# Attention and gated FFN on one core: whole-batch loads, attention by token tile over all heads, full-array matmuls, two-bank PSUM tiles, output tiles across batch pairs

## The chip, the cores and the metric

The kernel runs on one core of one Trainium2 chip. The metric is the device time of one execution in microseconds (us). The kernel before takes 329.29 us (median of 2 runs, 328.94 to 329.65). Every experiment below was timed beside runs of the kernel before on its own chip; those medians were 328.36, 329.02, 328.94 and 328.63 us, so the yardstick moves by 0.2%.

The engines are called as the profile calls them: PE is TensorE (matmuls), PEld its weight loads, ACT is ScalarE, DVE is VectorE, POOL is GpSimd, SP is SyncE. In both kernels matmuls write into tiles in the memory called PSUM, and an ACT or DVE instruction then moves each result into SBUF, where the other tiles lie; that instruction is called an eviction here. A two-bank tile is a PSUM tile of 2 x 512 float32 columns.

## The reference, cut to what matters

Eight batches, eight heads, 576 tokens, head size 64. K and V are averaged over groups of 8 tokens (72 pooled tokens), attention is taken over those, and a gated FFN with a convolution of three taps follows.

```python
k_p = k.reshape(B, H, 72, 8, 64).mean(axis=3)          # V likewise
attn = softmax(q @ k_p.T / 8)                          # 576 x 72 for each head
x = (attn @ v_p) joined over heads                     # 576 x 512
h = relu(x @ w_in)                                     # 576 x 1024
c = conv3(h, conv_w)                                   # along tokens, one filter per column
out = (h * sigmoid(c)) @ w_out                         # 576 x 512
```

## The kernel before

While the FFN of batch b runs, the attention of batch b+1 is woven between its blocks. The heads go in pairs. Each q row lands with token `c*96 + p` on partition p, so the transposed q has its tokens in order. A score matmul contracts over 64 rows (one head), between FFN matmuls that use all 128.

```python
def attn_loads(b, pr):
    ...
        for hh in range(2):
            nc.gpsimd.dma_start(
                out=q_sb[:, :, hh, :],
                in_=q[b, h0 + hh, :, :].rearrange("(c p) d -> p c d", p=96),
            )

def attn_scores(b, pr):
    ...
    for c2 in range(n_sc):              # two halves of 288 tokens
        c0 = c2 * SC
        for hh in range(2):
            pb = hh * D
            scps = sc_psum.tile([Sp, SC], FP32, name="scps", tag="sc")
            nc.tensor.matmul(
                out=scps,
                lhsT=kT_sb[pb:pb + D, :],            # 64 rows x 72 columns
                rhs=qT_sb[pb:pb + D, c0:c0 + SC],
                start=True, stop=True,
            )
            nc.scalar.activation(
                out=attnTs[hh][:, c0:c0 + SC], in_=scps, func=ACT.Exp, scale=1.0 / (POOL * 8.0)
            )

# the FFN: 16 times 4 matmuls of 288 columns (hps, relu by ACT), 16 times 3 (cps, tanh by ACT),
# then five output tiles of 128, 128, 128, 128 and 64 tokens, 8 matmuls of 512 columns each
... (the rest cut)
```

The softmax here doesn't subtract the row's maximum and nothing guards it: scores larger than these inputs give would overflow.

## Time and profile before

| read from | value |
|---|---|
| median time | 329.29 us (328.94 to 329.65) |
| span of the profiled execution | 327.8 us |
| PE busy | 289.7 us, 88% of the span |
| chain of waits, share of PE | 79% |
| one steady batch | 35.80 us, of which PE is busy 35.1, DVE 26.0, ACT 22.4 |

The table of stretches, for two steady batches (a third is equal) (from, to: length, then the busy time and count of PE, PEld, DVE, ACT and POOL, the granted TensorE clock, the busy share of the DMA engines and GB/s):

```profile
124.70:160.50 35.80, 35.06 (x259) 20.11 (x259) 25.79 (x113) 22.42 (x58) 12.21 (x23) 1.00 0.61 84
160.50:196.30 35.80, 35.21 (x265) 20.25 (x263) 26.05 (x114) 22.38 (x58) 12.50 (x24) 1.00 0.62 84
```

PE is busy for 98% of a batch. That is no proof that it does useful work all that time. The timeline of PE in one of these batches shows what a score matmul costs; the first number of a line is the start in us, the second the duration, and because matmuls overlap it is the distance between starts that counts.

```profile
128.28 0.28 PE L273 MATMUL hps<-xT,w_in_sb_116 128*128 128x288 bf16 x1
128.57 0.28 PE L191 MATMUL scps<-qT_sb,kT_sb 64*72 64x288 bf16 x1
128.79 0.30 PE L273 MATMUL hps<-xT,w_in_sb_117 128*128 128x288 bf16 x1
128.92 0.29 PE L273 MATMUL hps<-xT,w_in_sb_118 128*128 128x288 bf16 x1
```

Two 128-row matmuls in a row start 0.13 us apart (128.79, 128.92). With a 64-row score matmul between them they start 0.51 us apart (128.28, 128.79). PE counts as busy through all of it.

### The profile page before, as it was taken

To read this page: it belongs to the slowest core of one execution; us is meant where nothing else is said; L and a number is where in the kernel's file an instruction comes from. 1 tells how busy PE (TensorE), PEld (TensorE's weight loads), DVE (VectorE), ACT (ScalarE), POOL (GpSimd) and SP (SyncE) were. 2 spreads that over 40 slices of the span, in tenths; PEclk is the share of its full clock that TensorE was granted. 3 is DMA by queue.
4 is the path that set the end of the run, shared out by engine and by line. 5 is a ranking of instruction groups with operands and counts; after the bars stand their busy time and mean duration, and the time that the engine had idled before them with its cause. 6 is when DMAs were issued, how large, how long until landed. Compare 5 with 4: busy or idle time off the path is not lost.

```text
span 327.8 us, 6104 instructions
## 1 busy us (share of the span) xinstructions
PE 289.7 (88%) x2080; PEld 166.7 (51%) x2080; DVE 213.5 (65%) x904; ACT 188.3 (57%) x473; POOL 103.0 (31%) x196
## 2 busy tenths in 40 slices
PE   0054669999999999999999999999999999999995
PEld 0032335664566446654656456554566455645752
DVE  3523883677857785778757785777667866675452
ACT  1068425883398509872587429860787348852940
POOL 8068997752442226042513233110000000000000
PEclk9999999999999999999999999999999999999999
DMA  8999999995693659155964567133100120003003
GB/s 166 173 120 190 150 151 129 147 104 98 125 100 22 84 123 109 31 54 97 135 79 36 82 138 56 8 27 108 40 2 1 66 81 2 0 34 112 2 32 113
DMA packets 57342, 27.28 MB, mean 83 GB/s; under 512 B 42464, under 2 KB 51552, under 8 KB 57312
## 3 DMA queue, kind: packets, MB, share of 16 engines
q0 software_dynamic: 51968, 17.20, 48.2%
q10 hardware_dynamic: 2928, 5.38, 4.9%
q1 hardware_dynamic: 2416, 4.33, 4.5%
q8 instruction: 16, 0.26, 0.3%
q14 instruction: 14, 0.11, 0.1%
HBM read 32.52 MB, written 9.44 MB: 128 GB/s over the span
## 4 chain that ended last, share of the span: by engine, by line
PE 79%; DMA 11%; ACT 3%; DVE 3%; POOL 2%; issue 1%; ACTq 0%; POOLq 0%
PE hps L273 22%; PE cps L293 15%; PE scps L191 8%; DMA q_sb<-in_q_dram 5%; PE avps L223 5%; PE xt_ps L252 3%; PE q_ps L173 2%; DMA convw<-in_moe_conv_w_dram 2%; ACT xT L255 2%; DMA k_raw<-in_k_dram 2%; DMA w_in_sb_119<-in_moe_w_in_dram 1%; DVE osb L336 1%; DMA out_dram<-osb 1%; PE kT_ps L162 1%; DVE x_pair L234 1%
## 5 line engine op out<-in xcount | busy, mean ns | idle before, releaser
L234 DVE TENSOR_SCALAR x_pair<-avps,r_sb 128x64 bf16<-128x64 f32 (+1 forms) x320 | 72.3, 275 | 0.5
L293 PE MATMUL cps<-hT,dw 128*128 128x288 bf16 x384 | 60.3, 288 | 0.0
L255 ACT COPY xT<-xt_ps 128x576 bf16<-128x576 bf16 x32 | 20.4, 637 | 69.0 <-PE xt_ps L252 56.9
L121 POOL DMA_DIRECT2D q_sb<-in_q_dram x64 | 47.9, 759 | 35.7 <-PE q_ps L173 22.5
L231 DVE RECIPROCAL r_sb<-avps 128x2 f32<-128x2 f32 (+1 forms) x160 | 22.9, 161 | 54.4 <-PE avps L223 53.7
L198 ACT ACTIVATE attnT<-scps 72x288 bf16<-72x288 f32 x128 | 51.0, 405 | 12.8 <-PE scps L191 9.5
L280 ACT ACTIVATE hT<-hps 128x288 bf16<-128x288 f32 x128 | 52.0, 413 | 8.1 <-PE hps L273 3.7
L300 ACT ACTIVATE tg<-cps 128x288 bf16<-128x288 f32 x128 | 48.7, 412 | 7.4 <-PE cps L293 7.1
L191 PE MATMUL scps<-qT_sb,kT_sb 64*72 64x288 bf16 x128 | 39.1, 318 | 5.4 <-ACT attnT L198 4.8
L223 PE MATMUL avps<-v_aug,attnT 72*128 72x65 bf16 (+1 forms) x320 | 37.9, 202 | 5.3 <-DVE x_pair L234 4.2
L328 PEld LDWEIGHTS <-gT 128*128 128x128 bf16 (+1 forms) x320 | 27.8, 99 | 26.0 <-DVE gT L321 1.8
L293 PEld LDWEIGHTS <-dw 128*128 128x128 bf16 x384 | 35.3, 98 | 9.7 <-issue 0.2
L223 PEld LDWEIGHTS <-attnT 72*128 72x128 bf16 (+1 forms) x320 | 26.4, 102 | 26.0 <-issue 9.7
L273 PE MATMUL hps<-xT,w_in_sb_116 128*128 128x288 bf16 x128 | 37.5, 295 | 2.3 <-DVE osb L336 1.4
L273 PE MATMUL hps<-xT,w_in_sb_119 128*128 128x288 bf16 x128 | 36.4, 293 | 3.1 <-ACT xT L255 3.1
L273 PE MATMUL hps<-xT,w_in_sb_118 128*128 128x288 bf16 x128 | 37.5, 295 | 0.4 <-ACT xT L255 0.4
L273 PE MATMUL hps<-xT,w_in_sb_117 128*128 128x288 bf16 x128 | 37.4, 294 | 0.4 <-ACT xT L255 0.4
L178 ACT COPY qT_sb<-q_ps 128x576 bf16<-128x576 bf16 x32 | 20.5, 640 | 25.3 <-PE q_ps L173 25.1
L147 POOL MEMSET v_aug<- 72x2 bf16 x32 | 3.3, 110 | 100.2 <-PE avps L223 99.8
L191 PEld LDWEIGHTS <-kT_sb 64*72 64x72 bf16 x128 | 13.4, 109 | 29.2 <-issue 23.1
L252 PE MATMUL xt_ps<-ident_b,x_pair 128*128 128x128 bf16 (+1 forms) x160 | 26.5, 224 | 0.1
L113 POOL DMA_DIRECT2D v_raw<-in_v_dram x28 | 19.8, 707 | 11.5 <-DVE vt_3488 L149 2.6
(719 smaller groups left out, 429.3 us busy)
## 6 DMA issues: line engine op xcount, KB each, us to landing
q_sb<-in_q_dram POOLq DMA_DIRECT2D x64, 72.0 KB, 3.8
out_dram<-osb ACTq DMA_DIRECT2D x16, 256.0 KB
k_raw<-in_k_dram POOLq DMA_DIRECT2D x28, 144.0 KB, 4.5
v_raw<-in_v_dram POOLq DMA_DIRECT2D x28, 144.0 KB, 4.3
out_dram<-osb SPq DMA_DIRECT2D x8, 256.0 KB
out_dram<-osb POOLq DMA_DIRECT2D x8, 256.0 KB, 2.4
v_raw<-in_v_dram ACTq DMA_DIRECT2D x4, 288.0 KB
k_raw<-in_k_dram SPq DMA_DIRECT2D x4, 288.0 KB
```

What stands on the lines that cost most here:

```text
L121: nc.gpsimd.dma_start(out=q_sb[:, :, hh, :], in_=q[b, h0 + hh, :, :].rearrange("(c p) d -> p c d", p=96),)
L191: nc.tensor.matmul(out=scps, lhsT=kT_sb[pb:pb + D, :], rhs=qT_sb[pb:pb + D, c0:c0 + SC], start=True, stop=True,)
L198: nc.scalar.activation(out=attnTs[hh][:, c0:c0 + SC], in_=scps, func=ACT.Exp, scale=1.0 / (POOL * 8.0))
L223: nc.tensor.matmul(out=avt[0:usz, sl, hh, :], lhsT=attnTs[hh][:, u0:u0 + usz], rhs=v_aug[:, hh, :], start=True, stop=True,)
L234: nc.vector.tensor_scalar(out=x_pair[0:usz, hh * D:(hh + 1) * D], in0=avt[0:usz, sl, hh, 0:D], scalar1=r_sb[0:usz, hh:hh + 1], scalar2=Non ...
L252: nc.tensor.transpose(out=xt_ps[:, u0:u0 + usz], in_=x_pairs[i][0:usz], identity=ident_b[0:usz, 0:usz])
L255: nc.scalar.copy(out=xT, in_=xt_ps)
L273: nc.tensor.matmul(out=hps, lhsT=w_in_sb[dc][:, fb * P:(fb + 1) * P], rhs=xT_tiles[(b, dc)][:, c0:c0 + SC], start=(dc == 0), stop=(dc == n ...
L280: nc.scalar.activation(out=hT[:, fb, 1 + c0:1 + c0 + SC], in_=hps, func=ACT.Relu, scale=0.5)
L293: nc.tensor.matmul(out=cps, lhsT=dw[:, kk, i, :], rhs=hT[:, fb, c0 + kk:c0 + kk + SC], start=(kk == 0), stop=(kk == 2),)
L300: nc.scalar.activation(out=tg[:, c0:c0 + SC], in_=cps, func=ACT.Tanh, scale=0.5)
L328: nc.tensor.matmul(out=ops_[0:osz, :], lhsT=gT[:, fc, os0:os0 + osz], rhs=w_out_sb[fc], start=(fc == 0), stop=(fc == n_fb - 1),)
```

## The change

The intent is to give PE nothing but full-array matmuls and to give the other engines fewer and larger instructions.

- q, k and v of a whole batch come in one DMA each. For q, six consecutive tokens go to one partition (token `p*6 + c`), so a descriptor moves 1,536 contiguous bytes of float32 instead of 256.
- Keys are padded with zeros to 128 rows, and q is transposed two tokens at a time, so a score matmul is 128 rows deep. Its output is in the order of q's partitions; the exp puts the tokens back in order as it writes.
- Relu, tanh and exp evict 576 columns at once from two-bank PSUM tiles. Attention by V goes by token tile over four heads at a time; the last tile overlaps the one before, so that every tile has 128 tokens.
- Output tiles run over the 1,152 tokens of two batches: 9 full tiles in place of 10.
- The convolution's diagonal weights and the copies of the transposed q and x move from ACT to DVE, and every other output copy from DVE to ACT.

The core of the diff (cut; lines of the old and the new score function, the q load and the output tile):

```diff
-                in_=q[b, h0 + hh, :, :].rearrange("(c p) d -> p c d", p=96),
+    q_view = "h (p c) d -> p h c d"
+        nc.gpsimd.dma_start(out=qr, in_=q[b].rearrange(q_view, c=QC))
 ...
-                    lhsT=kT_sb[pb:pb + D, :],
-                    rhs=qT_sb[pb:pb + D, c0:c0 + SC],
-                nc.scalar.activation(
-                    out=attnTs[hh][:, c0:c0 + SC], in_=scps, func=ACT.Exp, scale=1.0 / (POOL * 8.0)
+        ps = big_psum.tile([P, 2, 512], FP32, name="sc_ps", tag="big")
+        for c2 in range(2):
+            nc.tensor.matmul(
+                out=ps[0:Sp, c2, 0:SC],
+                lhsT=kz[b % 2][:, h, c2, :],
+                rhs=qT[:, h % 2, :],
+        at = attnT_pool.tile([Sp, S], BF16, name="attnT")
 ...
+            nc.scalar.activation(
+                out=at.rearrange("s (p cp c2) -> s c2 cp p", cp=QC // 2, c2=2),
+                in_=ps[0:Sp, :, 0:SC].rearrange("s c2 (cp p) -> s c2 cp p", cp=QC // 2),
+                func=ACT.Exp,
+                scale=1.0 / (POOL * 8.0),
+            )
 ...
+                lhsT=gT[:, fb, j * P:(j + 1) * P],       # gT holds 2 * 576 tokens
+        tiles = range(0, 4) if b % 2 == 0 else range(4, 9)
 ... (the rest cut)
```

The output of the exp: token `p*6 + cp*2 + c2`, with p running fastest.

## The prediction

> **What bounds it now.** The chain of waits is 79% TensorE work. In time order it shows about 50 us of start-up, seven batches of 35.8 us (FFN of b, attention of b+1), and a last batch without attention of 22 us plus 3.6 us of tail. In a steady batch the table by stretches shows PE busy 35.1 of 35.8 us, DVE 26.1, ACT 22.4, clock 1.00; the waits list has 3.6 us of PE idle in six batches. TensorE bounds it.
>
> **Where the 35.8 us go.** In the timeline a 288-column matmul follows another every 0.123 us, a 512-column one every 0.216, a 128-column transpose every 0.058, a q transpose every 0.042. Dense, a batch costs 7.84 (first FFN matmul) + 5.88 (conv) + 8.64 (five output tiles) + 1.97 (scores) + about 3.8 of small work = 28 us. About 7.7 is lost: a score matmul on a 64-row tile between 128-row ones costs about 0.35 us, and 64-wide tails about 0.1 us at each change. The Trainium skill (TensorEngine Tiling, Key Properties) says that changing the tiling mode drains the engine; the trace agrees, about 60 changes x 0.11 us.
>
> **Per batch, after.** All matmuls take the full array, so about 6.6 us of changes goes. Output tiles: 4.5 in place of 5, -0.86 us. PE sum: 26.9 us (4 tiles) or 28.6 (5), mean 27.7. ACT: 24 evictions of 576 columns at about 0.65 us (the 576-column copy took 0.637) plus half the output copies: 17 us. DVE, from about 0.15 us fixed plus columns: trees 5.9, q copies 1.8, normalising 10 x 0.58, x copies 2.1, gate 8 x 0.77, output 1.5: 23 us. That is below PE but near it while AV runs, with two one-bank buffers for everything small: I allow 1.3 us of new waits, so about 29 us.
>
> **Start-up.** q descriptors of 256 B become 1,536 B. FFN 0 could begin near 30 us instead of 50. But the built order puts later trees early on DVE: K of batch 2 stands ahead of the last xT copy of batch 0, and K, V up to batch 5 ahead of batch 1. At about 330 GB/s read (estimate from packet durations), K of batch 2 lands near 45 us, and batch 0 is then paced by loads and eight trees. Most of the gain is given back: batch 1 starts near 80 us in place of 87.
>
> **Sum.** 80 + 6 x 29 + 22 + 3.6 = 280 of span; timed runs are 1.5 us above the span. Predicted **283 us**, range 268 to 302. Chances: faster by over 2% 0.96, within 2% 0.03, slower 0.01.
>
> **What would show it.** Right: steady period 28 to 30 us; scores on 128-row tiles at 0.123 us spacing; no 64-wide tiles; PE idle of 1 to 2 us per batch, released by DVE or ACT; DVE idle before trees released by DMA in the first 80 us. Wrong: period above 31 us with PE waiting for DVE or ACT (the two-buffer pool, or slow PSUM copies); or batch 1 near 60 us (loads faster than estimated, or the trees do not hold back FFN 0).
>
> **What would make it wrong.** bf16 copies from PSUM at half the assumed rate add 3 us of DVE per batch; three two-bank buffers shared by first matmul, conv and scores make PE wait for ACT; strided exp output slower than 0.65 us; the load rate.

## More of the kernel before

The page first. Its first part gives each engine's busy time and share of the span; part 4 is the chain of work that ended last; part 5 has groups of instructions, with the busy time in us and the mean time of one in ns after the first bar.

```profile
span 327.8 us, 6104 instructions
PE 289.7 (88%) x2080; PEld 166.7 (51%) x2080; DVE 213.5 (65%) x904; ACT 188.3 (57%) x473; POOL 103.0 (31%) x196
...
PE 79%; DMA 11%; ACT 3%; DVE 3%; POOL 2%; issue 1%; ACTq 0%; POOLq 0%
...
L198 ACT ACTIVATE attnT<-scps 72x288 bf16<-72x288 f32 x128 | 51.0, 405 | 12.8 <-PE scps L191 9.5
...
L191 PE MATMUL scps<-qT_sb,kT_sb 64*72 64x288 bf16 x128 | 39.1, 318 | 5.4 <-ACT attnT L198 4.8
```

The last work is almost all PE's, and ACT is on 3% of the chain only. The exps take 405 ns each, two for a head.

## The result, and the profile after

The changed kernel takes **356.49 us** (356.00 to 356.97, 2 runs). It is slower: the ratio to the kernel before is 1.083, with a 95% interval of 1.078 to 1.088. Ratios here are the mean time of one kernel's fast runs over that of the other's of the same rounds, so not quite the ratio of the medians that are quoted.

The same parts of the page, after:

```profile
span 355.1 us, 5143 instructions
PE 264.0 (74%) x2049; PEld 169.0 (48%) x2049; DVE 176.3 (50%) x497; ACT 210.4 (59%) x209; POOL 26.4 (7%) x55
...
ACT 40%; PE 37%; DVE 14%; issue 5%; DMA 3%; ACTq 0%
...
L182 ACT ACTIVATE attnT<-sc_ps 72x576 bf16<-72x576 f32 x64 | 128.0, 2216 | 13.4 <-PE sc_ps L165 13.4
...
L245 ACT ACTIVATE hT<-h_ps 128x576 bf16<-128x576 f32 x64 | 48.1, 754 | 36.9 <-PE h_ps L238 36.9
...
L265 ACT ACTIVATE tg<-c_ps 128x576 bf16<-128x576 f32 x64 | 41.9, 654 | 8.4 <-PE c_ps L257 4.7
```

PE's busy time did fall, by 26 us, and DVE's by 37. ACT was on 3% of the chain and is on 40% now. Three evictions of 576 columns stand side by side in part 5: relu 754 ns, tanh 654 ns, and exp 2,216 ns. The exp has the fewest partitions of the three.

Two steady batches in the table of stretches (the mean of six is 39.75 us, read from the first convolution matmul of each batch in the timeline):

```profile
132.34:171.09 38.75, 31.01 (x255) 20.10 (x253) 20.23 (x56) 25.99 (x26) 0.96 (x3) 0.96 0.19 43
171.09:211.56 40.47, 32.95 (x262) 20.81 (x261) 18.75 (x55) 26.01 (x26) 0.94 (x3) 0.96 0.19 48
```

No engine is busy for more than 82% of the batch, and ACT for two thirds only (25.99 of 38.75, 26.01 of 40.47). A share over the batch hides the stage that limits. The scores of the eight heads stand in four of the FFN's steps, two heads in each, and there the timelines of ACT and PE look as follows.

```profile
250.97 0.65 ACT L265 ACTIVATE tg<-c_ps 128x576 bf16<-128x576 f32 x1
251.51 4.00 ACT L182 ACTIVATE attnT<-sc_ps 72x576 bf16<-72x576 f32 x2
255.13 0.87 ACT L245 ACTIVATE hT<-h_ps 128x576 bf16<-128x576 f32 x1
255.88 0.65 ACT L265 ACTIVATE tg<-c_ps 128x576 bf16<-128x576 f32 x1
...
253.65 0.90 PE L257 MATMUL c_ps<-hT,dw 128*128 128x288 bf16 x6 [0.84 <-ACT attnT L182]
...
255.56 0.89 PE L165 MATMUL sc_ps<-qT,kz_107 128*72 128x288 bf16 x4 [0.76 <-ACT attnT L182]
```

A step takes 4.9 us (tanh at 250.97, the next at 255.88), ACT has no gap in it, and PE waits twice, 0.84 and 0.76 us, for an exp to free a PSUM buffer. The list of PE's waits over six batches (what waited, for what, us in total, times, longest) agrees:

```profile
PE c_ps L257 <- ACT attnT L182: 17.6, 21, 0.8
PE sc_ps L165 <- ACT attnT L182: 14.3, 18, 1.0
PE av_ps L195 <- ACT attnT L182: 5.5, 6, 1.0
```

The start-up pays as well: the chain of waits holds the first eight exps as one piece of 15.5 us.

So the question was what makes an exp of 576 columns take 2.2 us. Theory T1: the write, 2-byte elements 12 bytes apart. Rivals: the four-dimensional access pattern itself (T2), the stepped read or the two-bank source, and, for the time as a whole, the start-up alone or the change's pools.

### The profile page after: what moved, and what is told of

It reads as the page before. It is cut to its first block, busy times and chain, and to the rows that moved or that the text cites. A ratio compares the mean times of both kernels' runs of the same rounds, so it can differ in the third digit from the quotient of the medians.

```text
span 355.1 us, 5143 instructions
## 1 busy us (share of the span) xinstructions
PE 264.0 (74%) x2049; PEld 169.0 (48%) x2049; DVE 176.3 (50%) x497; ACT 210.4 (59%) x209; POOL 26.4 (7%) x55
## 4 chain that ended last, share of the span: by engine, by line
ACT 40%; PE 37%; DVE 14%; issue 5%; DMA 3%; ACTq 0%
ACT attnT L182 32%; PE o_ps L277 17%; PE h_ps L238 9%; PE c_ps L257 7%; ACT tg L265 4%; DVE x L206 4%; DMA v_126<-in_v_dram 3%; ACT hT L245 3%; PE av_ps L195 2%; DVE gT L271 2%; DVE o L288 2%; PE xt_ps L219 1%; DVE xT L221 1%; DVE r L205 1%; PE q_ps L152 1%
## 5 line engine op out<-in xcount | busy, mean ns | idle before, releaser
L182 ACT ACTIVATE attnT<-sc_ps 72x576 bf16<-72x576 f32 x64 | 128.0, 2216 | 13.4 <-PE sc_ps L165 13.4
L238 PE MATMUL h_ps<-xT,w_in_sb 128*128 128x288 bf16 x512 | 84.6, 304 | 2.0 <-DVE xT L221 0.5
L257 PE MATMUL c_ps<-hT,dw 128*128 128x288 bf16 x384 | 62.5, 295 | 20.3 <-ACT attnT L182 19.9
L245 ACT ACTIVATE hT<-h_ps 128x576 bf16<-128x576 f32 x64 | 48.1, 754 | 36.9 <-PE h_ps L238 36.9
L277 PE MATMUL o_ps<-w_out_sb,gT 128*128 128x512 bf16 x288 | 65.6, 382 | 5.7 <-DVE o L288 4.1
L238 PEld LDWEIGHTS <-w_in_sb 128*128 128x128 bf16 x512 | 49.6, 102 | 19.5 <-issue 5.9
L265 ACT ACTIVATE tg<-c_ps 128x576 bf16<-128x576 f32 x64 | 41.9, 654 | 8.4 <-PE c_ps L257 4.7
L277 PEld LDWEIGHTS <-gT 128*128 128x128 bf16 x288 | 27.6, 98 | 39.1 <-issue 6.0
L288 DVE COPY o<-o_ps 128x512 f32<-128x512 f32 x20 | 13.8, 691 | 44.2 <-PE o_ps L277 44.2
L206 DVE TENSOR_TENSOR x<-av_ps,r 128x256 bf16<-128x256 f32 x80 | 33.5, 419 | 0.8
L158 DVE COPY qT<-q_ps 128x576 bf16<-128x576 bf16 x32 | 14.6, 457 | 31.4 <-PE q_ps L152 31.0
L205 DVE RECIPROCAL r<-av_ps 128x4 f32<-128x4 f32 x80 | 13.8, 177 | 25.1 <-PE av_ps L195 24.4
L165 PE MATMUL sc_ps<-qT,kz_107 128*72 128x288 bf16 x64 | 14.3, 325 | 14.4 <-ACT attnT L182 8.5
L195 PE MATMUL av_ps<-va_109,attnT 72*128 72x65 bf16 x160 | 13.8, 208 | 11.8 <-ACT attnT L182 8.0
L165 PE MATMUL sc_ps<-qT,kz_108 128*72 128x288 bf16 x64 | 13.4, 304 | 10.6 <-ACT attnT L182 9.7
```

Of the source, the lines that this page charges most:

```text
L165: nc.tensor.matmul(out=ps[0:Sp, c2, 0:SC], lhsT=kz[b % 2][:, h, c2, :], rhs=qT[:, h % 2, :], start=True, stop=True,)
L182: nc.scalar.activation(out=at.rearrange("s (p cp c2) -> s c2 cp p", cp=QC // 2, c2=2), in_=ps[0:Sp, :, 0:SC].rearrange("s c2 (cp p) -> s c ...
L195: nc.tensor.matmul(out=ps[:, hh, :], lhsT=st[b]["at"][h][:, t0:t0 + P], rhs=va[b % 2][:, h, :], start=True, stop=True,)
L206: nc.vector.tensor_tensor(out=st[b]["x"][i][:, 4 * g:4 * g + 4, :], in0=ps[:, :, 0:D], in1=r.unsqueeze(2).to_broadcast([P, 4, D]), op=OP.mult,
L238: nc.tensor.matmul(out=ps[:, c, 0:SC], lhsT=w_in_sb[:, dc, fb * P:(fb + 1) * P], rhs=xT[:, dc, c * SC:(c + 1) * SC], start=(dc == 0), stop ...
L245: nc.scalar.activation(out=hT[:, fb, 1:S + 1].rearrange("p (c n) -> p c n", c=NS), in_=ps[:, :, 0:SC], func=ACT.Relu, scale=0.5,)
```

## The experiments

"Period" below is the distance between the first convolution matmuls of successive batches in the timeline. Batches alternate, because odd ones have five output tiles and even ones four.

| run | time, us (fast runs) | ratio to before, 95% | steady period, us |
|---|---|---|---|
| before | 329.29 | 1 | 35.8 |
| the change | 356.49 | 1.083 (1.078 to 1.088) | 39.75 mean |
| e1 exps in order | 288.86 | 0.881 (0.876 to 0.886) | 31.5 / 29.7 |
| e2 q rows apart | 294.33 | 0.898 (0.893 to 0.902) | 31.5 / 29.7 |
| e4 before, full array | 300.30 | 0.915 (0.911 to 0.919) | 31.5 mean |
| e5 half the exps slow | 316.87 | 0.962 (0.961 to 0.964) | not read |
| e6 five output tiles | 296.90 | 0.904 (0.901 to 0.906) | 31.5 |
| e7 trees held back | 322.74 | 0.981 (0.978 to 0.984) | 36.5 mean |
| e8 keys 128 wide | 294.51 | 0.894 (0.892 to 0.896) | 31.5 / 29.7 |
| e10 trees held by half a batch | 297.43 | 0.904 (0.901 to 0.907) | 32.8 / 32.2 |
| e11 = e1 again | 289.97 | 0.882 (0.879 to 0.885) | 31.5 / 29.7 |
| e12 before, spread exps | 394.76 | 1.199 (1.195 to 1.203) | 44.0 |
| e13 first trees held | 287.33 | 0.873 (0.869 to 0.876) | 31.4 / 29.6 |

All give the reference's result. e1 to e4 ran on one chip, e5 to e8 on a second, e10 to e12 on a third, and e13 later on the first. e6, e7, e8, e10 and e13 are e1 with one more edit, e4 and e12 the kernel before with one. e3 is a measurement inside a longer kernel (427.81 us, one run) and has no place in the table.

### e1: the exp writes in order and reads out of order

The output is walked in token order, and the same permutation is put on the PSUM side.

```diff
-                out=at.rearrange("s (p cp c2) -> s c2 cp p", cp=QC // 2, c2=2),
-                in_=ps[0:Sp, :, 0:SC].rearrange("s c2 (cp p) -> s c2 cp p", cp=QC // 2),
+                out=at.rearrange("s (p cp c2) -> s p cp c2", cp=QC // 2, c2=2),
+                in_=ps[0:Sp, :, 0:SC].rearrange("s c2 (cp p) -> s p cp c2", cp=QC // 2),
```

> The changed kernel with one edit: the exp eviction walks its output in order (step 1) and takes the reordering on the side of the PSUM read (innermost read step: one bank). Theory (T1): the 2-byte results written at a step of 6 elements are what made an exp of 576 columns take 2.2 us; with an output in order it takes about 0.65 us, ACT no longer sets the pace, the steady period falls from about 40 us to 28 to 30 us and the run to 270 to 290 us. Rival (T2): it is the four-dimensional pattern with short runs as such, or the crossing of two banks: exp stays above 1.5 us and the run above 335 us. Rival (T3): exp gets fast but the three two-bank buffers still hold PE back: exp at 0.65 us, period above 33 us.

Measured: 288.86 us (288.20 to 291.53), 67.6 us below the change and 12% below before. The lines of its page, and the two stretches:

```profile
PE 242.6 (85%) x2041; PEld 164.2 (57%) x2049; DVE 175.4 (61%) x497; ACT 128.6 (45%) x209; POOL 27.0 (9%) x55
...
L182 ACT ACTIVATE attnT<-sc_ps 72x576 bf16<-72x576 f32 x64 | 37.6, 639 | 17.4 <-PE sc_ps L165 17.4
```

```profile
171.88:201.49 29.61, 27.98 (x254) 19.32 (x253) 16.77 (x52) 15.83 (x26) 1.01 (x3) 1.00 0.24 57
140.44:171.88 31.44, 29.77 (x261) 20.11 (x261) 18.70 (x55) 15.87 (x26) 1.01 (x3) 1.00 0.25 62
```

The exp falls from 2,216 to 639 ns with the same elements moved, the same function and the same permutation, now on the other side. PE is busy for 95% of a batch again. ACT's 10 us per batch that went (26.0 to 15.85) and the 9.3 us by which the mean period fell (39.75 to 30.48) agree, and so does the step: 4.9 us in the change, 2.6 in the same timeline of e1, four times a batch, make 9.2. T3 falls with it: the three two-bank buffers are still there. The granted clock rose too, from 0.96 to 1.00 in the stretches shown; that was not tested by itself, but the four steps leave it little.

### e2: q rows loaded so that no reordering is needed

One DMA per head puts token `c*96 + p` on partition p; the exp then writes runs of 96 elements, through the change's number of dimensions.

```diff
-    q_view = "h (p c) d -> p h c d"
+    q_view = "(c p) d -> p c d"
-        nc.gpsimd.dma_start(out=qr, in_=q[b].rearrange(q_view, c=QC))      # the like for batch 0 cut
+        for hh in range(H):
+            nc.gpsimd.dma_start(out=qr[:, hh], in_=q[b, hh].rearrange(q_view, c=QC))
 ...
-                out=at.rearrange("s (p cp c2) -> s c2 cp p", cp=QC // 2, c2=2),
+                out=at.rearrange("s (cp c2 p) -> s c2 cp p", cp=QC // 2, c2=2),
```

> The changed kernel with the q load of the kernel before (rows 96 apart, 256-byte pieces, one DMA for each head), so that exp writes six runs of 96 neighbouring columns, read and write both at step 1 inside a run; the pattern stays four-dimensional. T1: exp about 0.65 us, period 28 to 30 us, the run within 3% of the run with exp in order; the small q pieces may cost it up to 5 us in start-up. T2 (four dimensions): exp stays above 1.5 us, above 335 us.

Measured: 294.33 us (293.74 to 296.90). T2 falls: a pattern of four dimensions with runs of 96 is fast. The steady periods equal those of e1; the 5 us more lie in the start-up (batch 0 takes 36.2 us against 33.2), where the 256-byte pieces of q are loaded. That these pieces are the cause is not shown: in e8 batch 0 takes as long without them.

### e3: output steps measured by themselves

After the change's last output tile the same 72x576 PSUM source is evicted three times in each of many forms, with nothing else running. The results go to scratch memory; the kernel's own output is right.

```diff
+    for _ in range(3):  # bf16 step 6; likewise 1, 2, 3, 4, 8, 16, and fp32
+        nc.scalar.activation(out=scr[:, 0:3456].rearrange("s (n k) -> s n k", k=6)[:, :, 0]..., in_=flat, func=ACT.Exp, scale=1.0 / 64.0)
+    ... (as the change; as the change with Relu; gather as e1; runs of 96; DVE copies)
```

> The changed kernel, and after its last output tile a row of evictions by themselves, three of each form, 72x576 from PSUM: ACT exp to bf16 at output steps 1, 2, 3, 4, 6, 8, 16, to fp32 at steps 1, 2, 6, the form of the change with exp and with relu, the form with output in order, the form with runs of 96, an SBUF read at step 6, and DVE copies. T1: duration 0.65 us at step 1 and growing with the output step up to a plateau near 2.2 us at 12 bytes and more; the form with output in order and the runs of 96 near 0.65; relu as slow as exp. T2: the form with output in order as slow as the change. Open: whether fp32 results at a step are slow too (if it is a matter of 2-byte writes they are not), and whether DVE pays the same. The whole run about 30 us longer than the changed kernel; that time says nothing.

Measured, in the groups of its profile (L426 to L438 are bf16 with steps of 1, 2, 3, 4, 6, 8 and 16 elements; L444 is float32 with a step of 6; L448 is the change's pattern with Relu, L450 that of e1; L458 and L462 are DVE copies with the patterns of the change and of e1):

```profile
L426 ACT ACTIVATE gT<-src_ps 72x576 bf16<-72x576 f32 x3 | 1.9, 646 | 3.7 <-DVE tg L421 3.6
L428 ACT ACTIVATE gT<-src_ps 72x576 bf16<-72x576 f32 x3 | 2.4, 804 | 0.1
L430 ACT ACTIVATE gT<-src_ps 72x576 bf16<-72x576 f32 x3 | 3.4, 1122 | 0.1
L434 ACT ACTIVATE gT<-src_ps 72x576 bf16<-72x576 f32 x3 | 6.2, 2075 | 0.1
L436 ACT ACTIVATE gT<-src_ps 72x576 bf16<-72x576 f32 x3 | 8.1, 2709 | 0.1
L438 ACT ACTIVATE gT<-src_ps 72x576 bf16<-72x576 f32 x3 | 7.7, 2567 | 0.1
L444 ACT ACTIVATE gT<-src_ps 72x576 f32<-72x576 f32 x3 | 3.5, 1166 | 0.1
L448 ACT ACTIVATE gT<-src_ps 72x576 bf16<-72x576 f32 x3 | 6.2, 2072 | 0.1
L450 ACT ACTIVATE gT<-src_ps 72x576 bf16<-72x576 f32 x3 | 1.9, 646 | 0.1
L458 DVE CAST gT<-src_ps 72x576 bf16<-72x576 f32 x3 | 6.2, 2062 | 60.9 <-ACT gT L456 60.8
L462 DVE CAST gT<-src_ps 72x576 bf16<-72x576 f32 x3 | 2.3, 753 | 0.1
```

For these bf16 outputs the step of the output sets the time. Relu pays as much as exp, DVE as much as ACT, and the scattered read from PSUM nothing. Of the forms not shown above, step 4 took 1,438 ns, the change's own pattern with exp 2,084, runs of 96 took 646, float32 outputs with steps of 1, 2 and 6 took 746, 671 and 1,166, and a read of 96 elements from SBUF with a step of 6 took 328 in place of 283. From step 2 to step 8 each further element of step adds about 0.32 us to the 576 columns, and at 16 it is no more than at 8.

Sixteen bytes are 8 bf16 elements. The Trainium skill (SBUF — State Buffer, Door 1: The DMA port swizzle, the note on cachelines) says that SBUF has 16-byte cachelines, that each access that crosses to a new line pays a penalty, and that one may stride for free up to 8 bf16. An estimate from the measured times and the page's line size: 0.17 us plus 4.4 ns for each 16-byte line that a write enters. With a step of 6 the output enters 576 x 12 / 16 = 432 lines, 2.07 us (measured 2.075); with 8, 576 lines, 2.70 us (2.709); with 3, 216 lines, 1.12 us (1.122); with 2, 144 lines, 0.80 us (0.804). With 1 it would give 0.49, less than the 0.646 that the elements themselves take. With 16 the sum is again 2.70, and 2.567 was measured. The two constants are fitted to these times, so that lines are the cause is argued and not shown. The plateau at 8 agrees with the line of 16 bytes; "for free up to 8" does not agree for these writes. The float32 write with step 6 enters a new line with every element too and took 1.17 us, so the cost of a line is higher for the 2-byte writes; why was not tested.

### e4: the full array alone, put into the kernel before

Keys padded with zeros to 128 rows, doubled transposes of the keys, the last token tile as one of 128; everything else as before.

```diff
-                    lhsT=kT_sb[pb:pb + D, :],
-                    rhs=qT_sb[pb:pb + D, c0:c0 + SC],
+                    lhsT=kT_sb[:, hh, :],            # 128 rows, the other head's 64 are zero
+                    rhs=qT_sb[:, c0:c0 + SC],
 ... (transposes, the last token tile and its output copy cut)
```

> The kernel before with only the full-array part of the change: zero-padded keys, so that the score matmuls read 128 rows, keys transposed in doubled form, and the last token tile of 64 taken as 128 with the overlap written once. Loads, evictions, pools, five output tiles per batch as before. My theory of the 7.7 us lost per batch (about 60 changes of tile shape at 0.11 us): the period falls from 35.8 to 29 to 30 us, scores stand 0.123 us apart, and the run is 280 to 292 us. Rival: the gaps beside the scores come from something else (waits on ACT, weight loads); then the period stays above 34 us and the run above 320 us. In between (period 31 to 33): ACT or DVE become the next limit at 22 and 26 us busy.

Measured: 300.30 us (299.44 to 301.61), a mean period of 31.5 us. The idea of the change is good: 4.3 of the 7.7 us per batch that I had put down to changes of tile shape come back. ACT and DVE are not the next limit, as PE waits for them 3.0 us in six batches. The timeline shows a part of what stays:

```profile
181.85 0.28 PE L280 MATMUL hps<-xT,w_in_sb 128*128 128x288 bf16 x1
182.15 0.28 PE L198 MATMUL scps<-qT_sb,kz 128*72 128x288 bf16 x1
182.27 0.41 PE L280 MATMUL hps<-xT,w_in_sb 128*128 128x288 bf16 x2
182.52 0.28 PE L198 MATMUL scps<-qT_sb,kz 128*72 128x288 bf16 x1
182.64 0.28 PE L280 MATMUL hps<-xT,w_in_sb 128*128 128x288 bf16 x1
182.92 0.28 PE L198 MATMUL scps<-qT_sb,kz 128*72 128x288 bf16 x1
```

After a score matmul the next starts 0.12 us later, as it should. A score matmul that follows a single FFN matmul starts 0.28 to 0.30 us after it (181.85 to 182.15, 182.64 to 182.92). One that follows two loses nothing: the three together take 0.37 us (182.27 to 182.64).

### e5: half the exps slow

```diff
+            if h % 2:
+                (the exp as in e1)
+            else:
+                (the exp as in the change)
```

> The change with the exps of the odd heads writing in order (0.64 us) and those of the even heads writing 6 elements apart as the change does (about 2.1 us); every step of the FFN that holds scores has one of each. T1 (the sum of ScalarE's work in a step sets the step: relu 0.75, tanh 0.54, one slow exp 1.8 from start to start, one fast 0.53): 3.6 us in a step, between 2.6 with none slow and 4.9 with two; the batch about 35 us, against 30.4 with none and 40 with all; whole run 315 to 325 us. Rival (a two-bank PSUM buffer held for the long time of any one slow exp stalls TensorE as much as two do): near the change's 356 us. Rival (only the first exps at the start matter): within 5 us of 289.

Measured: 316.87 us (316.32 to 316.90 in three fast runs). The profiled execution took 624.37 us and is left out, so there is no period to read. Of the 67 us between no slow exp and all slow, half of them cost 28 (316.87 less 288.86), a share of 0.41. T1's sum for a step gives (3.6 - 2.6) / (4.9 - 2.6) = 0.43. The share mixes chips: on this run's own chip e8, whose steady batches are those of e1, took 294.51 us, and against it half the exps cost 22. The rival that a single slow exp per step stalls PE as much as two do, and the one that only the first exps matter, both fall.

### e6: no output tiles across batches

```diff
-                lhsT=gT[:, fb, j * P:(j + 1) * P],
+                lhsT=gT[:, fb, (b % 2) * S + tok0[j]:(b % 2) * S + tok0[j] + P],
 ...
-        tiles = range(0, 4) if b % 2 == 0 else range(4, 9)
+        tiles = range(5)
```

> The version with in-order exps, but five output tiles of 128 tokens for each batch, the last overlapping the one before, in place of nine for two batches; still full tiles. My sum for the pairing: half a tile of 4 matmuls of 512 columns at 0.216 us, 0.86 us of TensorE per batch; 8 batches, of which the even ones get one tile more and the odd ones none, so 4 tiles x 1.73 = 6.9 us in all: 295 to 296 us against 288.9. Rival (TensorE has waits near the output tiles anyway, so the extra tile fills them): less than 3 us.

Measured: 296.90 us. The steady periods are 31.5 us; with the pairing they alternate between 31.5 and 29.7. Half of 1.8 us is 0.9 per batch, against my 0.86. Of the 8 us to e1, 5.4 lie in batches 2, 4 and 6, and 2.6 in batch 0 (35.8 against 33.2 us). Batch 0 has one tile more here too, but e8 on the same chip shows a long batch 0 (36.2 us) without this edit, so how its 2.6 us divide between tile and start-up is not shown.

### e7: the K and V trees held back

Here the rest of the prediction is tested, the start-up. In the change, the addition trees for K and V of batches 1 and 2 stand on DVE ahead of the last copies of x of batch 0. A copy of one element of the hidden tile into the tree's first buffer holds each tree back.

```diff
-    def tree(raw, n, dst):
+    def tree(raw, n, dst, gate=None):
+        if gate is not None:
+            nc.vector.tensor_copy(out=t1[0:1, 0, 0, 0:1], in_=gate)
 ... (gate of batch b: hT of batch b-1, block 0 for K and block 1 for V)
```

> The version with in-order exps, in which the K and V trees of batch b+1 first copy one element of batch b's hidden tile, so no tree can stand ahead of batch b's attention on VectorE in the start-up. My start-up theory (the trees of batches 1 and 2, waiting for loads, delay the last x copies of batch 0 and the first FFN): the FFN of batch 0 starts near 34 us in place of 43, the FFN of batch 1 near 64 to 70 in place of 79; in return VectorE has its trees back in each steady batch (about 5 us more, still below TensorE); whole run 275 to 283 us. Rival (the loads of batch 1 pace the start, whichever order VectorE has): FFN 0 earlier, batch 1 still near 79, whole run 287 to 292 us.

Measured: 322.74 us, so far off both expectations (the verdict is unclear, as the interval reaches across the 2%). One half was right: the first convolution of batch 0 starts at 39.4 us in place of 45.8, and that of batch 1 at 75.7 in place of 79.0, though 64 to 70 had been expected. But every later batch is about 6 us longer, 36.5 in place of 30.5. The chain of waits at the beginning of a batch shows why (start, us, what; only the longer pieces):

```profile
112.08 0.67 ACT hT L249
...
112.94 1.22 DVE t L126
...
115.37 0.59 DVE kdup L130
...
118.37 0.66 PE q_ps L156 x6
```

My gate put the K tree between the first hidden block and the key transposes of the same batch, and PE stood still for it. The list of PE's waits from 110 to 262 us has 8.9 us for the K tree's result and 6.4 us for the padded keys, where e1 has none: 3.8 of the 6 us per batch, in four batches. Trees that run ahead of their batch are not only a burden on the start. The granted clock of this run was also lower, 0.946 against 0.988 in e1; I did not separate that part.

### e8: keys 128 columns wide

The Trainium skill (TensorE: Matmul & The Clock Gate, Weight-path perf modes) says that fast weight loads are on when the number of weights is 128 and the type is not FP32. The padded keys have 72.

```diff
-    kz = [const_pool.tile([P, H, 2, Sp], BF16, name=f"kz{i}") for i in range(2)]
+    kz = [const_pool.tile([P, H, 2, P], BF16, name=f"kz{i}") for i in range(2)]
 ... (copies into kz and the score output's 128 rows cut)
```

> The version with in-order exps, with the zero-padded keys widened from 72 to 128 columns, so that the weights of a score matmul are 128x128. If the 72-column weights cost the extra (score matmuls stand 0.163 us apart, a 72-column weight load takes 0.122 us in the profile): 0.123 apart, 16 a batch, 0.6 to 1.0 us per batch, 284 to 286 us. Rival (the extra lies in the wait for the two-bank buffer or in the drain between kinds of matmul, or is hidden): no change, within 1.5 us of 288.9.

Measured: 294.51 us, and the periods are those of e1 to 0.03 us. The first pair of lines is of e1, the second of e8 (timeline of PE, four score matmuls and what follows):

```profile
177.95 0.66 PE L165 MATMUL sc_ps<-qT,kz 128*72 128x288 bf16 x4
178.59 1.14 PE L238 MATMUL h_ps<-xT,w_in_sb 128*128 128x288 bf16 x8
```

```profile
183.88 0.66 PE L165 MATMUL sc_ps<-qT,kz 128*128 128x288 bf16 x4
184.53 1.14 PE L238 MATMUL h_ps<-xT,w_in_sb 128*128 128x288 bf16 x8
```

Four take 0.64 and 0.65 us, 0.16 each, with 72 columns and with 128. The weight load itself did get shorter, from 122 to 102 ns in the mean, which agrees with the page; but the width is not what makes a score matmul cost 0.16 in place of 0.12 us. What does stays open. The 5.6 us to e1 lie before the first batch's end (36.2 us for batch 0), on a chip where the K loads took 15.2 us from issue to landing (median of seven) against 13.8 in e1. That the loads are the cause is not shown: e6 on the same chip took 14.7, and its batch 1 began at 81.1 us against 85.0 in e8.

### e11: e1 once more, beside the next two

> The version with in-order exps once more, unchanged, beside the next two on one chip: the first run of it stood on another chip than the five-tile, held-back and wide-key versions, whose first batch took 2.6 to 3.0 us longer while their steady batches did not. If that is the chip's load rate, this run gives 289 to 295 us with steady batches of 31.5 and 29.6 us as before.

Measured: 289.97 us (289.10 to 290.84), ratio 0.882 against 0.881, periods unchanged. The result of e1 holds on another chip. Why the start was longer on the second chip stays open, as this run was not made there.

### e10: the trees run ahead by half a batch

```diff
+        gate = st[0]["xT"][0:1, 0, S - 1:S] if b == 1 else st[b - 2]["hT"][0:1, 3, 1:2]   # K; block 5 for V
```

> As the held-back version, but the trees of batch 1 wait only for the last x copy of batch 0, and those of batch b from 2 on for the middle of the FFN of batch b-2 (hidden blocks 3 and 5), so they run ahead by half a batch and not by several. My theory of the held-back version (its gate put the K tree between the first hidden block and the score matmuls of the same batch, about 6 us of TensorE waiting per batch, while the start-up did gain 6 us): FFN 0 again starts near 38 us, steady batches are 30 to 31 us again, batch 1 starts near 72 in place of 79; 280 to 285 us, 5 to 8 us below the in-order version of the same call. Rival (trees that run far ahead are needed to keep VectorE off TensorE's path in every batch): steady batches above 33 us, no gain over the in-order version.

Measured: 297.43 us, 7.5 us above e11. The early start is there again (first convolution of batch 0 at 39.1 us), but most of it is lost at once: PE then waits 2.8 us for the first K tree and 0.7 for its keys, and that of batch 1 starts at 78.4 us against e11's 80.5. The steady batches are 32.8 and 32.2 us, in between the two expectations, though nearer to the rival's: a tree in the middle of a batch falls among the normalising instructions, and PE's waits for x are 8.0 us from 110 to 262 us (4.4 before the next product with V, 3.6 before the x transposes), against 4.2 in e1 and e11. The granted clock was 0.964, against 0.982 in e11, which I did not separate.

### e12: the spread write alone, put into the kernel before

```diff
-                in_=q[b, h0 + hh, :, :].rearrange("(c p) d -> p c d", p=96),
+                in_=q[b, h0 + hh, :, :].rearrange("(p c) d -> p c d", p=96),
 ...
-                    out=attnTs[hh][:, c0:c0 + SC], in_=scps, func=ACT.Exp, scale=1.0 / (POOL * 8.0)
+                    out=attnTs[hh].rearrange("s (p c) -> s c p", c=6)[:, 3 * c2:3 * c2 + 3],
+                    in_=scps.rearrange("s (c p) -> s c p", c=3), func=ACT.Exp, scale=1.0 / (POOL * 8.0)
```

> The kernel before, with one part of the change alone: q rows loaded 6 consecutive tokens to a partition, and so exps that write 288 bf16 elements 6 apart (correct result). T1[...]: one exp takes about 1.1 us in place of 0.405, 16 a batch add 11 us to ScalarE's 22.4 of a batch of 35.8 us, so ScalarE nearly reaches TensorE: a batch of 37 to 40 us; the start-up is some us shorter by the larger q descriptors; whole run 330 to 350 us. Rival (the slow write needs something else of the change, such as the two-bank source or 576 columns at once): exp near 0.4 us, the run below before's 329 us by the start-up's gain.

Measured: 394.76 us (393.54 to 396.01), 66 us above before. The exp's group and one steady batch:

```profile
L198 ACT ACTIVATE attnT<-scps 72x288 bf16<-72x288 f32 x128 | 131.9, 1238 | 4.2 <-PE scps L191 3.2
```

```profile
189.71:233.75 44.04, 37.69 (x261) 20.53 (x261) 26.30 (x114) 31.86 (x57) 13.24 (x24) 0.96 0.51 68
```

The direction is T1's, the exp goes from 405 ns to 1,238 (1,097 to 1,383), and the rivals that need two banks or 576 columns fall. The size of the whole was wrong again, and in the same way as in the prediction. I had compared ACT's sum (33 us) with PE's (35.8) over the batch. ACT is busy 31.9 of 44.0 us and yet costs 8.2: the scores fill some stretches, where ACT limits, and the rest of the batch cannot make up for them. PE's idle time is 5.6 us of the 8.2 (6.35 against 0.74 us a batch). Its busy time also rose by 2.6 us, at a granted clock of 0.96 in place of 1.00; these two I did not take apart.

### e13: only the first trees held back

```diff
+        gate = st[0]["hT"][0:1, 3, 1:2] if b == 2 else None                  # K
+        gate = st[0]["hT"][0:1, 4 * b - 3, 1:2] if b <= 2 else None          # V
```

> The in-order version with three trees alone held back: V of batch 1 until hidden block 1 of batch 0, K of batch 2 until block 3, V of batch 2 until block 5; K of batch 1 and all later trees stand where they stood. If the start-up theory is right and the two held-back versions lost only because they held K of the coming batch, or the trees of every batch: FFN 0 starts at 38 to 40 us in place of 43.5 to 45, batch 1's first conv at 74 to 77 in place of 79 to 80.5, later batches 31.5 and 29.6 us as in the in-order version; 283 to 287 us, ratio to before about 0.867. Rival (the trees of later batches, moved out of the start, cost as much in FFN 0 and after as they gave): 288 to 291 us, ratio 0.88.

Measured: 287.33 us (286.83 to 287.88), ratio 0.873, the fastest of all. It lies between the two expectations. The first convolution of batch 0 starts at 44.0 us (45.8 and 46.7 in e1 and e11), that of batch 1 at 77.4 (79.0 and 80.5), and batch 1 takes 32.35 us instead of 31.5: a part of what the start gains is paid back, as I read it by the moved trees. The order of the trees in the start-up is worth 1.5 us against e1 on the same chip and 2.6 against e11, not the 6 that the earlier start of FFN 0 promised. The intervals of the ratios of e13 and e1 just touch, so this gain is hardly above the noise.

## Why the prediction was wrong, point by point

**The step that failed** is the term "ACT: 24 evictions of 576 columns at about 0.65 us". Sixteen of the 24, the relus and tanhs, took 0.754 and 0.654 us (0.653 and 0.650 in e1, so for them the figure was right). The eight exps took 2.2 us, 1.8 from start to start. I had taken 0.65 from a copy of the same size that writes in order (0.637), without looking at the order of the exp's output. e3 gives the missing term (2.07 us for this pattern alone), e1 removes it and with it 67.6 us, e5, with half the exps slow, gives 0.41 of it (28 of 67.6 us, across two chips), and e12 shows that it is enough by itself.

**"Strided exp output slower than 0.65 us" was named as a risk** and given no number. With one, "within 2%" and "slower" could not have been left at 4% together: ACT's sum for a batch would have been 26 us, and the sum of one step (relu 0.75, tanh 0.54, two exps 3.6) at 4.9 us against PE's 2.6. What the prediction named as a sign of being wrong did come, a period above 31 us with PE waiting for ACT, but for another reason than the two it gave: e1 has the same buffers and the same PSUM reads and is fast.

**What bounds the kernel before: right in kind, too large in size.** Full tiles in the kernel before (e4) recovered 4.3 of the 7.7 us per batch. The Trainium skill (TensorEngine Tiling, Key Properties) says that a change of the tiling mode drains TensorE; the trace fits that for the 64-row score matmuls (0.51 us from one FFN matmul to the next with a score matmul between them, in the lines shown), but e4's lines still have 0.42 where a single FFN matmul stands before a full-array score matmul, so a change of mode is not the only cost there, and my 60 changes of 0.11 us are not shown.

**The period without the slow exp: right to about 5%.** Predicted 29 us; e1 shows 30.5. PE is busy 28.9 us of it (predicted 27.7) and waits about 1.6 (predicted 1.3). The score matmuls at 0.16 in place of 0.123 us explain 0.6 of the PE term (16 x 0.04); the rest I did not take apart.

**Output tiles across pairs: right.** 0.86 us per batch predicted, 0.9 in e6.

**The start-up: right in place, and partly in cause.** Batch 1 was to start near 80 us; its first convolution is at 79.0 and 80.5 in e1 and e11, and at 91.6 in the change, where the first eight exps alone stand on the chain for 15.5 us. The trees do hold back FFN 0 by 6 to 8 us (e7, e10), but freeing it brought batch 1 only 1.6 to 3.3 us forward (e7, e10, e13). That 80 us was met within 1 us is partly luck: with the same order of trees batch 1 began at 85.0 us in e8 and 83.3 in e2.

**The sum.** 283 us was predicted. The change without its spread write takes 288.9, and the change itself 356.5, outside the range of 268 to 302.

What stays open: why a score matmul takes 0.16 us between full tiles, why the 2-byte write pays more with its step than the 4-byte one and whether lines are the reason, why the start is longer in some runs, and how much of e7's loss is its lower clock.

## What to carry to other kernels

Cost an instruction by its access pattern and not by its size alone: where a layout change for one engine (larger descriptors, deeper matmuls) leaves a permutation to be done, put the permutation on the side that pays nothing for it, which here was the PSUM read and not the 2-byte SBUF write. Judge an engine in the stage where its work stands and not by its share of the batch: ACT was busy for two thirds of the batch, limited four steps of it, and cost 9 us per batch. And give every risk that you name a number before you give it a chance.

## What the Trainium skill lacked or had wrong

- SBUF — State Buffer (the note on cachelines, in Door 1: The DMA port swizzle) lets one stride for free up to 8 bf16. For bf16 writes of 72x576 elements by ACT the cost begins at step 2 and grows to step 8: 646, 804, 1,122, 1,438, 2,075 and 2,709 ns at steps 1, 2, 3, 4, 6 and 8, then 2,567 at step 16. The plateau fits the page's 16 bytes; e1's scattered read from PSUM with an output in order cost nothing (646 ns).
- ScalarE: Activation LUTs (What ACT_TABLE_LOAD costs) gives 186 ns + 0.833 ns per column for an ACTIVATE with immediate scale and bias, whatever the function, fp32 and bf16 alike. That is an estimate of 666 ns for 576 columns, against 646 measured, and holds for bf16 outputs in order only: a float32 output in order took 746 ns, and the same ACTIVATE took 2,075 ns with an output step of 6. The page doesn't mention the output's pattern.
- Vector Engine (DVE) Microarchitecture Reference (5.2 Measured stream behaviour on trn2, the SBUF access granule) measures stepped writes of 4-byte words, 2.50 ns per column at worst against 1.054. A bf16 copy from PSUM with the change's output pattern took 2,062 ns for 576 columns, 3.6 ns per column, against 753 ns in order; the page has no 2-byte stepped write.
- TensorE: Matmul & The Clock Gate (Weight-path perf modes) ties fast weight loads to 128 weights. Score matmuls with 72 and with 128 weight columns started 0.16 us apart alike (e8), though the load was shorter with 128 (102 ns against 122). I found no page that tells why they cost more than the 0.12 us of their neighbours.
